# Attention followed by a mixture of experts: routing's GpSimd operations spread over the steps, and two VectorE operations fewer per routing

## The chip, the cores and the metric

The kernel runs on one core of a Trainium2 chip (trn2). The core has TensorE (PE in the profile; its weight loads are shown apart as PEld), VectorE (DVE), ScalarE (ACT), GpSimd (POOL) and SyncE (SP), which issues most of the DMAs. GpSimd issues the DMAs whose rows are addressed by an index (indirect DMAs). The metric is the device time of one execution in microseconds, lower is better.

## The reference

Four batches of 12288 queries attend to a pooled key/value image; every result row (49152 rows of 128) then goes through a gated choice of one of eight experts.

```python
kv_pool = kv.reshape(B, H // r, r, W // r, r, C).mean(axis=(2, 4))
k = v = kv_pool.reshape(B, -1, C) @ w_sr            # 768 keys per batch
a = softmax(scale * q @ k.T);  x = a @ v
do_compute = x @ w_skip > 0
logits = x[do_compute] @ w_gate                     # 8 experts
e_idx = argmax(logits);  gate_w = softmax(logits)[e_idx]
for e in range(E):                                  # rows of expert e
    y[mask] = gate_w[mask, None] * (relu(x[mask] @ w1[e]) @ w2[e])
out = x;  out[do_compute] += y
```

## The kernel before

**Steps.** The attention is one unrolled loop of 384 steps (96 per batch), one tile of 128 queries each. A step on TensorE is six score matmuls (L588 to L590, into one of two `s_ps` buffers), eighteen matmuls that apply the probabilities of the tile six steps back (`attend`, L653) and two transposes (L628). VectorE takes the row maximum of the scores (`row_max`, L596, out tile `nm`), then ScalarE the exponential (L602), then VectorE the low half of the probabilities (`p_lo`, L610, which reads two SBUF tensors); in odd steps VectorE also has L636, L661 and L663, and in every fourth step the low half of the queries (L575, two SBUF tensors). SyncE transposes the probabilities by DMA.

**Routing.** `route` is a generator for twelve tiles at a time (one `r`). A `yield 0` or `yield 3` parks it until the step number has that remainder mod 4, a bare `yield` until the next step. With `slots` (all but the last few) its parts fall into steps whose remainder mod 12 is, by r's own clock: 8 (VectorE: logits times the columns' scales, L703, and their maximum, L705; GpSimd: L707 to L723, six operations that give `d`, `ev`, `act`, `na`), 0 (VectorE L733 and L735, GpSimd the one-hot `oh_all`, L736), 3 (two matmuls that count rows, L768 and L769), 4 (VectorE L745, L774, L777, GpSimd L778 to L782, four operations) and 8 again (VectorE L784, L791, L793: the row addresses `di`; GpSimd L794 and L795). From there GpSimd issues one scatter a step for twelve steps (L184 into `scr`): each waits for that step's `row_max`. Routings overlap, so from step 32 on there is a scatter in nearly every step.

**Pooling of the next batch.** In three of four batches GpSimd also sums the key/value image of the next batch (`pool_kv`, L436 and L439), one operation a step in eight steps of twelve. Each is made to wait for the last VectorE instruction noted in `paced["both"]`, one that reads two SBUF tensors (`behind`). `KV_T` says in which step each quarter of a key/value tile is loaded.

**Order.** Each engine runs its instructions in the order in which this code emits them; nothing reorders. At step 84 of a batch the next batch's keys are made on TensorE (`prep_kv`). After the attention come the experts (from about 1080 us).

Of the kernel before, what the change touches and what calls it, by code (L numbers as in the profile page):

```python
# [9 lines left out]
F32 = mybir.dt.float32  # L10
# [14 lines left out]
def kernel(  # L25
# [343 lines left out]
    with ExitStack() as p1:  # L369
# [13 lines left out]
        def acc_ps():  # L383
            return ps_a.tile([P, 512], F32, name="acc_ps")
# [120 lines left out]
        def prep_gate():  # L505
            n = XW - C
            ps = acc_ps()
            pa = kprep.tile([P, n], F32, name="pa")
            nc.vector.scalar_tensor_tensor(out=pa, in0=proj, scalar=-1.0, in1=proj, op0=ALU.mult, op1=ALU.max)
            nc.tensor.matmul(ps[:, :n], ones_f, pa, start=True, stop=True)  # L510
            yield
            l1 = kprep.tile([P, n], F32, name="l1")
            nc.vector.tensor_copy(l1, ps[:, :n])
            inv = pow2_inverse(l1, n, gate_ds)
            nc.vector.scalar_tensor_tensor(out=pa, in0=proj, scalar=0.25, in1=inv, op0=ALU.mult, op1=ALU.mult)
            ps = acc_ps()
# [34 lines left out]
        q_sb, qT, PT, AVT, ROWS, P_SB, S_PS, P16, PTP, PTQ = ({} for _ in range(10))  # L551
        accs, scales, snaps = {}, [], []
        split_a, split_v, next_a, next_v, next_l = [], [], [], [], []
# [127 lines left out]
        def route(r, a, b, last, eng):  # L681
            n = b - a
            rows = ROWS[r][:, a:b, :]
            L = rt.tile([P, RT, E], F32, name="lg")[:, 0:n, :]
            S3 = [P, n, E]
            x_sc = KV[r * RT // TPB][5]

            def small_t(name, dt=F32):
                return rt.tile([P, RT], dt, name=name)[:, 0:n]

            def big_t(name, dt=F32):
                return rt.tile([P, RT, E], dt, name=name)[:, 0:n, :]

# [5 lines left out]

            slots = r < LASTR - 3  # L700
# [9 lines left out]
            na = small_t("na")  # L710
            few = eng is nc.vector
            if few:
                eng.scalar_tensor_tensor(out=ev, in0=d, scalar=0.0, in1=em(em8), op0=ALU.is_equal, op1=ALU.mult)
                eng.tensor_scalar(out=act, in0=rows[:, :, C], scalar1=0.0, scalar2=None, op0=ALU.is_gt)
                eng.scalar_tensor_tensor(out=na, in0=rows[:, :, C], scalar=0.0, in1=idt[:, 0:n], op0=ALU.is_le,
                                         op1=ALU.mult)
                ohb = oh_few[a // GT % 2]
            else:
                eng.tensor_scalar(out=ev, in0=d, scalar1=0.0, scalar2=None, op0=ALU.is_equal)
                eng.tensor_tensor(out=ev, in0=ev, in1=em(em8), op=ALU.mult)  # L720
                eng.tensor_scalar(out=act, in0=rows[:, :, C], scalar1=0.0, scalar2=None, op0=ALU.is_gt)
                eng.tensor_scalar(out=na, in0=act, scalar1=-1.0, scalar2=1.0, op0=ALU.mult, op1=ALU.add)
                eng.tensor_tensor(out=na, in0=na, in1=idt[:, 0:n], op=ALU.mult)  # L723
                oha = oh_all[r % 3]
                ohb = oha.rearrange("p e t -> p t e")[:, 1:RTP, :]
            yield (0 if slots else None)
            if not few and not slots:
                for _ in range(3 if r < LASTR - 1 else K1):
# [21 lines left out]
            w = n * E  # L750
            acc = big_t("acc")
            nxt = ends if last else rt.tile([P, E], F32, name="nxt")
# [12 lines left out]
            else:  # L765
# [11 lines left out]
                nc.vector.tensor_tensor(out=acc, in0=inner, in1=pre.rearrange("p e t -> p t e")[:, 0:RT, :], op=ALU.add)  # L777
                eng.tensor_tensor(out=nxt, in0=run, in1=pre[:, :, RT], op=ALU.add)  # L778
                eng.tensor_scalar(out=gs, in0=gs, scalar1=1e-9, scalar2=x_sc, op0=ALU.add, op1=ALU.mult)
                eng.tensor_tensor(out=acc, in0=acc, in1=em(run), op=ALU.add)  # L780
            accs["done"] = r * RT + b
            eng.tensor_tensor(out=acc, in0=acc, in1=ohb[:, 0:n, :], op=ALU.mult)  # L782
# [4 lines left out]
            if r == SNAPR:  # L787
                snapshot(accs["run"])
# [3 lines left out]
            di = small_t("di", I32)  # L792
            nc.vector.tensor_tensor(out=di, in0=dest, in1=na, op=ALU.add)  # L793
            nc.gpsimd.tensor_copy(rows[:, :, C + 2], x_sc.broadcast_to([P, n]))  # L794
            nc.gpsimd.iota(rows.bitcast(I32)[:, :, C + 1], pattern=[[1, n]], base=r * RT * P + a, channel_multiplier=RT)  # L795
            for j in range(n):
                if j > 0 and r < LASTR - 1:
# [135 lines left out]
        while t < NTILE + LAG - 1 or jobs:  # L933
# [44 lines left out]
            if ph == 1 and t // GT + 2 < NGRP:  # L978
                q_split(t // GT + 2)
            ranked = run_jobs(ph)  # L980
            if preps and not ranked and (ph != 0 or tb < LAG):
                if next(preps[0], "end") == "end":
                    preps.pop(0)
            if live and b + 1 < B:
                for k, r in KV_T.get(tb - 4, ()):
                    if r == R - 1:
                        pools.append(pool_kv(b + 1, k))
                if pools and next(pools[0], "end") == "end":
                    pools.pop(0)
            for _ in range(2 * (t >= NTILE)):  # L990
                next(first)
# [77 lines left out]
```

## Time and profile before

| | |
|---|---|
| median of 3 runs | 1887.3 us (1886.7 to 1890.96) |
| the profiled execution, its own time | 1881.36 us |
| its span, first to last instruction | 1878.9 us |
| PE busy | 1758.9 us, 94% |
| DVE busy | 1570.0 us, 84% |
| POOL busy | 1009.5 us, 54% |

The shares are means over the attention (to about 1030 us), a passage of some 50 us, and the experts. A stretch is read best by its own rows.

### The profile page before, as it was taken

What the parts mean: (1) busy time and instruction counts of PE and PEld (TensorE: products, weight loads), DVE (VectorE), ACT (ScalarE), POOL (GpSimd) and SP (SyncE); (2) the same over time, 40 slices, a digit from 0 to 9 for tenths busy, and PEclk for the clock granted to TensorE, in tenths of its full rate; (3) what the DMA queues carried; (4) which work ended last, traced back from release to release, by engine and by line L of the source; (5) the groups of instructions that cost most, each with busy time, mean ns of one, the idle gap of its engine ahead of it and who ended that gap; (6) DMA issues with size and microseconds to landing.
All of it is one profiled execution on the core that took longest, in us unless ns stands there. A gap on an engine that the chain in (4) does not pass through costs nothing. (4 is left out here: it accounts for less than half of the span.)

```text
span 1878.9 us, 42842 instructions
## 1 busy us (share of the span) xinstructions
PE 1758.9 (94%) x13955; PEld 1259.9 (67%) x13955; DVE 1570.0 (84%) x3322; ACT 1312.4 (70%) x2484; POOL 1009.5 (54%) x1276
## 2 busy tenths in 40 slices
PE   4999999999999999999999669999999999999997
PEld 3988889888888888899988324444444444444443
DVE  7998989998899898999997458878878877877885
ACT  3888878887878787888877236566666666666654
POOL 2168857887757888565566623433333433343343
PEclk9999999999999999999999879999999999999998
DMA  6999999999899999999998333433333333333333
GB/s 180 206 205 211 206 188 224 205 187 185 159 183 184 210 206 197 186 229 221 220 205 175 80 84 80 107 101 101 93 94 101 93 93 101 91 93 97 96 106 79
DMA packets 621972, 284.88 MB, mean 152 GB/s; under 512 B 503168, under 2 KB 571904, under 8 KB 621824
## 3 DMA queue, kind: packets, MB, share of 16 engines
q1 hardware_dynamic: 600320, 244.56, 64.6%
q0 software_dynamic: 21504, 38.43, 7.0%
q8 instruction: 82, 1.34, 0.3%
q14 instruction: 66, 0.54, 0.1%
HBM read 90.60 MB, written 78.64 MB: 90 GB/s over the span
## 5 line engine op out<-in xcount | busy, mean ns | idle before, releaser
L184 POOL DMA_INDIRECT out_dram<-o,xin x288 | 292.8, 1017 | 505.0 <-DVE o L293 438.9
L184 POOL DMA_INDIRECT scr<-rows,di x384 | 422.8, 1101 | 229.6 <-DVE nm L596 125.7
L270 DVE SCALAR_TENSOR_TENSOR h_lo<-h_ps,h_hi 128x512 f16<-128x512 f32 x544 | 341.0, 683 | 148.6 <-ACT h_hi L269 113.5
L602 ACT ACTIVATE p_sb<-s_ps,nm 128x768 f32<-128x768 f32 x384 | 346.3, 902 | 155.1 <-DVE nm L596 137.9
L596 DVE TENSOR_REDUCE nm<-s_ps 128x1 f32<-128x768 f32 x384 | 364.9, 950 | 65.4 <-PE s_ps L590 36.1
L269 ACT ACTIVATE h_hi<-h_ps 128x512 f16<-128x512 f32 x544 | 310.3, 597 | 50.5 <-PE h_ps L268 31.1
L653 PE MATMUL acc_ps<-v_hi,pt 128*128 128x138 f16 x3072 | 324.1, 225 | 18.5 <-issue 7.3
L653 PEld LDWEIGHTS <-pt 128*128 128x128 f16 x4608 | 277.6, 98 | 88.2 <-issue 82.9
L653 PE MATMUL acc_ps<-v_lo,pt 128*128 128x138 f16 x1536 | 295.3, 224 | 2.5 <-issue 2.4
L588 PE MATMUL s_ps<-k_hi,q_hi 128*128 128x384 f32 x768 | 295.4, 385 | 2.1 <-issue 2.1
L610 DVE SCALAR_TENSOR_TENSOR p<-p_sb,p 128x512 f16<-128x512 f32 x384 | 275.8, 718 | 2.6 <-DMA pt<-p 1.3
L589 PE MATMUL s_ps<-k_lo,q_hi 128*128 128x384 f32 x768 | 260.9, 340 | 0.7 <-issue 0.7
L590 PE MATMUL s_ps<-k_hi,q_lo 128*128 128x384 f32 x768 | 260.1, 339 | 1.2 <-issue 1.2
L606 ACT ACTIVATE p<-p_sb 128x512 f16<-128x512 f32 x384 | 242.4, 631 | 9.1 <-DMA pt<-p 6.2
L266 PE MATMUL h_ps<-xT,w_hi 128*128 128x512 f16 x544 | 206.8, 380 | 7.4 <-issue 7.4
L285 ACT ACTIVATE yT<-y_ps,y_sc 128x512 f32<-128x512 f32 x68 | 46.7, 687 | 230.4 <-PE y_ps L282 220.2
L267 PE MATMUL h_ps<-xT,w_hi 128*128 128x512 f16 x544 | 206.7, 380 | 0.0
L268 PE MATMUL h_ps<-xT,w_lo 128*128 128x512 f16 x544 | 206.7, 380 | 0.0
L282 PE MATMUL y_ps<-h_hi,w_hi 128*128 128x512 f16 x544 | 206.2, 379 | 0.0
L282 PE MATMUL y_ps<-h_hi,w_lo 128*128 128x512 f16 x544 | 206.2, 379 | 0.0
L282 PEld LDWEIGHTS <-w_hi 128*128 128x128 f16 x1152 | 112.8, 98 | 132.6 <-issue 0.8
L282 PE MATMUL y_ps<-h_lo,w_hi 128*128 128x512 f16 x544 | 195.1, 379 | 0.0
(208 smaller groups left out, 3128.5 us busy)
## 6 DMA issues: line engine op xcount, KB each, us to landing
kvt<-in_kv_dram SPq DMA_DIRECT2D x96, 256.0 KB
q_sb<-in_q_dram SPq DMA_DIRECT2D x96, 256.0 KB
out_dram<-rows SPq DMA_DIRECT2D x96, 256.0 KB
xin<-scr SPq DMA_DIRECT2D x75, 264.0 KB, 2.9
w_raw<-in_moe_w_dram SPq DMA_DIRECT2D x38, 512.0 KB
scr<-pad SPq DMA_DIRECT2D x32, 264.0 KB
pt<-p SPq DMA_TRANSPOSE x384
scr<-rows,di POOLq DMA_INDIRECT x384
```

Source lines behind the costliest of these rows:

```text
L184: ins = nc.gpsimd.indirect_dma_start(out=dst, out_offset=bass.IndirectOffsetOnAxis(ap=ids, axis=0), in_=src, in_offset=None, bounds_check= ...
L269: nc.scalar.activation(out=h["hi"][:, c, :], in_=ps, func=AF.Relu)
L270: nc.vector.scalar_tensor_tensor(out=h["lo"][:, c, :], in0=ps, scalar=0.0, in1=h["hi"][:, c, :], op0=ALU.max, op1=ALU.subtract)
L282: nc.tensor.matmul(ps, w[:, c, :], h[x][:, c, :], start=(i == 0), stop=(i == len(terms) - 1))
L588: nc.tensor.matmul(s[:, h, :HK], q_hi, k_hi[:, sl], start=True, stop=False)
L589: nc.tensor.matmul(s[:, h, :HK], q_hi, k_lo[:, sl], start=False, stop=False)
L590: nc.tensor.matmul(s[:, h, :HK], q_lo, k_hi[:, sl], start=False, stop=True)
L596: paced["by"] = nc.vector.tensor_reduce(out=NM[t], in_=S_PS[t][:, :, :HK], axis=AX.XY, op=ALU.max, negate=True).ins
L602: nc.scalar.activation(out=P_SB[t], in_=S_PS.pop(t)[:, :, :HK], func=AF.Exp, bias=NM.pop(t))
L606: nc.scalar.activation(out=P16[t][:, 0, :], in_=p_flat(t)[:, 0:KD * P], func=AF.Copy, scale=2.0 ** PEXP)
L610: paced["both"] = nc.vector.scalar_tensor_tensor(out=p16[:, 1, :], in0=p_flat(t)[:, 0:KD * P], scalar=2.0 ** PEXP, in1=p16[:, 0, :], op0=A ...
L653: nc.tensor.matmul(ps[:, j % 2, :], w, v[a][:, k, :], start=(i == 0), stop=(i == len(AVL) - 1))
```

## The change

Five edits. (1) The eight columns of the gate share one power of two as scale (`prep_gate`), so the logits are read straight from `rows`, the exponential takes the scale, and VectorE's L703 goes. (2) The term `na` that sends inactive rows out of bounds becomes a ninth column of `acc`, written by one GpSimd operation in place of two; VectorE takes the row address as the maximum of nine columns, straight into the integer tile `di`, in place of a sum and an addition. (3) In routings with `slots`, GpSimd's operations go through `pool`, which makes each wait for `paced["both"]` and notes it in `taken`; extra yields put at most two into a step, a step or more later than before. The scatters begin one step later (remainder 9). (4) `pool_kv` skips a step in which two were taken (until step 70 of a batch). (5) The key/value quarters are loaded every 2.5 steps in place of 3.

```diff
@@ prep_gate
             nc.vector.tensor_copy(l1, ps[:, :n])
+            nc.vector.tensor_reduce(out=l1[:, 1:2], in_=ps[:, 1:1 + E], axis=AX.X, op=ALU.max)
             inv = pow2_inverse(l1, n, gate_ds)
             nc.vector.scalar_tensor_tensor(out=pa, in0=proj, scalar=0.25, in1=inv, op0=ALU.mult, op1=ALU.mult)
+            nc.vector.tensor_scalar(out=pa[:, 1:1 + E], in0=proj[:, 1:1 + E], scalar1=inv[:, 1:2], scalar2=0.25,
+                                    op0=ALU.mult, op1=ALU.mult)
@@ route
-            L = rt.tile([P, RT, E], F32, name="lg")[:, 0:n, :]
+            def pool(name, **args):
+                op = getattr(eng, name)(**args)
+                if slots:
+                    behind(op)
+                    taken.append(name)
...
-            nc.vector.tensor_tensor(out=L, in0=rows[:, :, C + 1:C + 1 + E], in1=em(gate_ds[:, 1:1 + E]), op=ALU.mult)
+            L = rows[:, :, C + 1:C + 1 + E]
...
-            eng.tensor_tensor(out=d, in0=L, in1=bc(mx), op=ALU.subtract)
+            acc_n = big_t("acc", w=E + 1)
+            acc, na = acc_n[:, :, 0:E], acc_n[:, :, E]
+            if slots:
+                yield
+            pool("tensor_tensor", out=d, in0=L, in1=bc(mx), op=ALU.subtract)
...
+                pool("tensor_scalar", out=ev, in0=d, scalar1=0.0, scalar2=None, op0=ALU.is_equal)
+                if slots:
+                    yield
+                pool("tensor_tensor", out=ev, in0=ev, in1=em(em8), op=ALU.mult)
+                pool("tensor_scalar", out=act, in0=rows[:, :, C], scalar1=0.0, scalar2=None, op0=ALU.is_gt)
+                if slots:
+                    yield
+                pool("tensor_scalar", out=na, in0=act, scalar1=-float(BIG), scalar2=float(BIG), op0=ALU.mult,
+                     op1=ALU.add)
...
-            nc.scalar.activation(out=ex, in_=d, func=AF.Exp)
+            nc.scalar.activation(out=ex, in_=d, func=AF.Exp, scale=gate_ds[:, 1:2])
+            if slots:
+                yield 0
...
-            eng.tensor_tensor(out=ohb[:, 0:n, :], in0=oh, in1=bc(act), op=ALU.mult)
+            if slots:
+                yield
+            pool("tensor_tensor", out=ohb[:, 0:n, :], in0=oh, in1=bc(act), op=ALU.mult)
...
-            dest = small_t("dest")
-            nc.vector.tensor_reduce(out=dest, in_=acc, axis=AX.X, op=ALU.add)
             di = small_t("di", I32)
-            nc.vector.tensor_tensor(out=di, in0=dest, in1=na, op=ALU.add)
+            nc.vector.tensor_reduce(out=di, in_=acc_n, axis=AX.X, op=ALU.max)
+            if slots:
+                yield
@@ main loop
-            KV_T.setdefault(i * 3, []).append(divmod(i, R))
+            KV_T.setdefault(i * 5 // 2, []).append(divmod(i, R))
...
+            taken.clear()
...
-                if pools and next(pools[0], "end") == "end":
+                if pools and (len(taken) < 2 or tb >= 70) and next(pools[0], "end") == "end":
```

The first place where instructions move is GpSimd's queue around the start of a routing (`d` to `oh_all`; `scr` is the scatters' target, `kvt` the pooling). Before:

```order
L794 COPY rows<-x_sc 128x12
L795 IOTA rows 128x12
L184 DMA scr<-rows,di 409600x132
L707 TENSOR_TENSOR d<-lg,mx 128x96
L719 TENSOR_SCALAR ev<-d 128x96
L720 TENSOR_TENSOR ev<-ev,em_80 128x96
L721 TENSOR_SCALAR act<-rows 128x12
L722 TENSOR_SCALAR na<-act 128x12
L723 TENSOR_TENSOR na<-na,idt 128x12
L439 TENSOR_TENSOR pooled<-kvt 128x128
L184 DMA scr<-rows,di 409600x132 x4
L736 TENSOR_TENSOR oh_all_94<-oh,act 128x12x8
```

The same place on GpSimd in the changed kernel (L705 is the helper `pool`):

```order
L812 COPY rows<-x_sc 128x12
L813 IOTA rows 128x12
L184 DMA scr<-rows,di 409600x132
L705 TENSOR_TENSOR d<-rows,mx 128x96
L705 TENSOR_SCALAR ev<-d 128x96
L184 DMA scr<-rows,di 409600x132
L705 TENSOR_TENSOR ev<-ev,em_80 128x96
L705 TENSOR_SCALAR act<-rows 128x12
L184 DMA scr<-rows,di 409600x132
L705 TENSOR_SCALAR acc<-act 128x12
L436 TENSOR_TENSOR kvt<-kvt 128x256
L184 DMA scr<-rows,di 409600x132
```

Six operations and a pooling stood together ahead of four scatters in a row; now a scatter stands between every two operations, and no two scatters follow each other here.

The second place is VectorE's queue in the step with remainder 8 (`p` is `p_lo`). Before:

```order
L784 RECIPROCAL rows<-gs 128x12
L791 TENSOR_REDUCE dest<-acc 128x12
L793 TENSOR_TENSOR di<-dest,na 128x12
L703 TENSOR_TENSOR lg<-rows,gate_ds 128x96
L705 TENSOR_REDUCE mx<-lg 128x12
```

The same place on VectorE in the changed kernel:

```order
L805 RECIPROCAL rows<-gs 128x12
L809 TENSOR_REDUCE di<-acc 128x12
L714 TENSOR_REDUCE mx<-rows 128x12
L599 TENSOR_REDUCE nm<-s_ps 128x1
L639 SCALAR_TENSOR_TENSOR ptq<-acc_ps,ptq 128x512
```

Two of five routing instructions are gone there. TensorE's instructions and their order are the same in both kernels.

## Rows read from the trace of the kernel before

**Rows 1.** The page's head: span, busy time, share of the span and instructions of each engine.

```profile
span 1878.9 us, 42842 instructions
...
PE 1758.9 (94%) x13955; PEld 1259.9 (67%) x13955; DVE 1570.0 (84%) x3322; ACT 1312.4 (70%) x2484; POOL 1009.5 (54%) x1276
```

**Rows 2.** Windows of twelve steps each, cut at TensorE's first score matmul, in which TensorE waits for nothing: from:to and length in us, then busy us and instructions of PE, PEld, DVE, ACT and POOL, granted clock, the DMA engines' busy share and what they moved in GB/s. The first lies before any routing, the others hold one.

```profile
60.55:88.95 28.40, 28.40 (x314) 26.47 (x313) 25.75 (x48) 24.81 (x46) 7.81 (x14) 1.00 1.06 211
...
529.45:558.05 28.60, 28.60 (x317) 26.66 (x315) 27.52 (x57) 25.15 (x48) 16.91 (x24) 1.00 1.02 190
782.23:810.85 28.62, 28.62 (x316) 26.71 (x315) 27.73 (x57) 25.04 (x48) 17.04 (x24) 1.00 1.06 210
```

**Rows 3.** Stretches of 48, 72, 72 and 48 steps, the line of a step's first and fourth score matmuls alone (two a step): from:to, length, busy us and instructions of PE and PEld, clock, DMA.

```profile
117.53:240.85 123.32, 36.55 (x96) 18.13 (x96) 1.00 1.06 209
306.07:491.52 185.45, 54.80 (x144) 27.19 (x145) 1.00 1.02 192
558.05:744.17 186.12, 54.70 (x144) 27.19 (x144) 1.00 1.04 201
810.85:928.53 117.68, 36.53 (x96) 18.13 (x97) 1.00 1.11 222
```

**Rows 4.** Three more windows of twelve steps, columns as in the windows above: one with pooling, one without that holds the snapshot (a handful of VectorE operations more), and the one with most DMA traffic.

```profile
428.85:460.09 31.24, 29.51 (x316) 26.86 (x315) 28.19 (x56) 25.06 (x47) 25.34 (x35) 1.00 1.03 186
...
898.31:928.53 30.22, 29.10 (x317) 26.77 (x316) 27.44 (x64) 24.33 (x45) 16.75 (x25) 1.00 1.10 218
928.53:957.13 28.60, 28.60 (x315) 26.67 (x315) 28.13 (x59) 25.80 (x49) 18.30 (x26) 1.00 1.11 233
```

**Rows 5.** VectorE in order of time: start, duration, line, operation, tiles, and in brackets the idle time before and what ended it.

```profile
432.97 0.26 DVE L735 TENSOR_TENSOR oh<-em,mn 128x96 f32<-128x96 f32 x1
435.93 0.96 DVE L596 TENSOR_REDUCE nm<-s_ps 128x1 f32<-128x768 f32 x1 [2.70 <-PE s_ps L590]
...
437.73 0.69 DVE L610 SCALAR_TENSOR_TENSOR p<-p_sb,p 128x512 f16<-128x512 f32 x1
```

**Rows 6.** GpSimd in order of time over the same steps.

```profile
424.71 1.02 POOL L184 DMA_INDIRECT scr<-rows,di  x1 [0.56 <-POOL rows L795]
...
429.22 0.47 POOL L439 TENSOR_TENSOR pooled<-kvt 128x128 f32<-128x128 f32 x1
429.84 1.08 POOL L184 DMA_INDIRECT scr<-rows,di  x1 [0.16 <-DVE nm L596]
431.23 0.97 POOL L184 DMA_INDIRECT scr<-rows,di  x1 [0.30 <-issue]
432.50 1.12 POOL L184 DMA_INDIRECT scr<-rows,di  x1 [0.30 <-DVE nm L596]
433.93 0.97 POOL L184 DMA_INDIRECT scr<-rows,di  x1 [0.30 <-issue]
434.90 0.63 POOL L736 TENSOR_TENSOR oh_all<-oh,act 128x96 bf16<-128x96 f32 x1
```

**Rows 7.** GpSimd in order of time some steps earlier, between two routings' parts.

```profile
378.01 0.99 POOL L184 DMA_INDIRECT scr<-rows,di  x1 [0.17 <-issue]
...
380.34 1.19 POOL L184 DMA_INDIRECT scr<-rows,di  x1 [0.33 <-DVE nm L596]
```

**Rows 8.** TensorE in order of time (the ends of matmuls are modelled).

```profile
434.58 0.34 PE L590 MATMUL s_ps<-k_hi,q_lo 128*128 128x384 f32 x1
435.13 0.22 PE L653 MATMUL acc_ps<-v_hi,pt 128*128 128x138 f16 x1 [0.21 <-issue]
435.88 0.22 PE L653 MATMUL acc_ps<-v_hi,pt 128*128 128x138 f16 x1 [0.53 <-issue]
...
440.55 0.21 PE L768 MATMUL acc_ps<-oh_all,ones_bf 128*128 128x104 bf16 x1
```

**Rows 9.** VectorE and GpSimd together in order of time, where a pooling and a VectorE operation on two SBUF tensors meet.

```profile
353.03 0.74 POOL L436 TENSOR_TENSOR kvt<-kvt 128x256 f32<-128x256 f32 x1
...
353.11 1.20 DVE L610 SCALAR_TENSOR_TENSOR p<-p_sb,p 128x512 f16<-128x512 f32 x1
...
355.28 1.13 POOL L436 TENSOR_TENSOR kvt<-kvt 128x256 f32<-128x256 f32 x1
...
355.75 1.21 DVE L575 TENSOR_TENSOR q_lo<-q_sb,q_hi 128x512 fp32r<-128x512 f32 x1
```

**Rows 10.** The same VectorE operation where GpSimd is between scatters, in order of time.

```profile
855.85 0.69 DVE L610 SCALAR_TENSOR_TENSOR p<-p_sb,p 128x512 f16<-128x512 f32 x1
```

**Rows 11.** `row_max` in the first nine us of each of the three stretches in which the next batch's keys are made (240.85:250, 491.52:500.5 and 744.17:753): count, busy us, mean ns, and VectorE's idle us before it.

```profile
L596 DVE TENSOR_REDUCE nm<-s_ps 128x1 f32<-128x768 f32 x3 | 2.9, 951 | 3.0 <-remote 3.0
...
L596 DVE TENSOR_REDUCE nm<-s_ps 128x1 f32<-128x768 f32 x3 | 2.9, 951 | 2.7 <-remote 2.7
...
L596 DVE TENSOR_REDUCE nm<-s_ps 128x1 f32<-128x768 f32 x3 | 2.9, 951 | 2.9 <-remote 2.9
```

**Rows 12.** Groups of instructions: line, engine, operation, tiles, shapes, count, busy us, mean ns, idle us before.

```profile
L184 POOL DMA_INDIRECT scr<-rows,di x384 | 422.8, 1101 | 229.6 <-DVE nm L596 125.7 <-issue 67.5 <-DVE rs L663 8.6
...
L610 DVE SCALAR_TENSOR_TENSOR p<-p_sb,p 128x512 f16<-128x512 f32 x384 | 275.8, 718 | 2.6 <-DMA pt<-p 1.3 <-ACT p L606 1.1
...
L793 DVE TENSOR_TENSOR di<-dest,na 128x12 int32<-128x12 f32 x31 | 8.2, 265 | 1.1
...
L703 DVE TENSOR_TENSOR lg<-rows,gate_ds 128x96 f32<-128x96 f32 x31 | 7.7, 250 | 0.0
```

More of the change, by code (lines that the diff above doesn't have):

```diff
@@ L551 @@
         q_sb, qT, PT, AVT, ROWS, P_SB, S_PS, P16, PTP, PTQ = ({} for _ in range(10))
-        accs, scales, snaps = {}, [], []
+        accs, scales, snaps, taken = {}, [], [], []
         split_a, split_v, next_a, next_v, next_l = [], [], [], [], []
@@ L683, in route, with big_t @@
             rows = ROWS[r][:, a:b, :]
-            L = rt.tile([P, RT, E], F32, name="lg")[:, 0:n, :]
             S3 = [P, n, E]
             x_sc = KV[r * RT // TPB][5]
+            few = eng is nc.vector
+            slots = r < LASTR - 3
             def small_t(name, dt=F32):
                 return rt.tile([P, RT], dt, name=name)[:, 0:n]
-            def big_t(name, dt=F32):
-                return rt.tile([P, RT, E], dt, name=name)[:, 0:n, :]
+            def big_t(name, dt=F32, w=E):
+                return rt.tile([P, RT, w], dt, name=name)[:, 0:n, :]
             def bc(x):
@@ L698, in em @@
                 return x.unsqueeze(1).broadcast_to(S3)
-            slots = r < LASTR - 3
+            def pool(name, **args):
[3 more added lines that the diff above has]
+                    taken.append(name)
             if slots:
                 yield 0
-            nc.vector.tensor_tensor(out=L, in0=rows[:, :, C + 1:C + 1 + E], in1=em(gate_ds[:, 1:1 + E]), op=ALU.mult)
+            L = rows[:, :, C + 1:C + 1 + E]
             mx = small_t("mx")
@@ L706, in route @@
             d = big_t("d")
-            eng.tensor_tensor(out=d, in0=L, in1=bc(mx), op=ALU.subtract)
             ev = big_t("ev")
             act = small_t("act")
-            na = small_t("na")
-            few = eng is nc.vector
+            acc_n = big_t("acc", w=E + 1)
+            acc, na = acc_n[:, :, 0:E], acc_n[:, :, E]
+            ohb = oh_few[a // GT % 2]
+            if slots:
+                yield
+            pool("tensor_tensor", out=d, in0=L, in1=bc(mx), op=ALU.subtract)
             if few:
@@ L716, in route @@
                                          op1=ALU.mult)
-                ohb = oh_few[a // GT % 2]
             else:
[L719 to L723, printed above, removed]
+                pool("tensor_scalar", out=ev, in0=d, scalar1=0.0, scalar2=None, op0=ALU.is_equal)
[7 more added lines that the diff above has]
+                     op1=ALU.add)
                 oha = oh_all[r % 3]
                 ohb = oha.rearrange("p e t -> p t e")[:, 1:RTP, :]
-            yield (0 if slots else None)
-            if not few and not slots:
-                for _ in range(3 if r < LASTR - 1 else K1):
+            if not slots:
+                for _ in range(1 if few else 4 if r < LASTR - 1 else 1 + K1):
                     yield
             ex = big_t("ex")
-            nc.scalar.activation(out=ex, in_=d, func=AF.Exp)
+            nc.scalar.activation(out=ex, in_=d, func=AF.Exp, scale=gate_ds[:, 1:2])
+            if slots:
+                yield 0
             mn = small_t("mn")
@@ L750, in route @@
             w = n * E
-            acc = big_t("acc")
             nxt = ends if last else rt.tile([P, E], F32, name="nxt")
@@ L777, in route @@
                 nc.vector.tensor_tensor(out=acc, in0=inner, in1=pre.rearrange("p e t -> p t e")[:, 0:RT, :], op=ALU.add)
-                eng.tensor_tensor(out=nxt, in0=run, in1=pre[:, :, RT], op=ALU.add)
-                eng.tensor_scalar(out=gs, in0=gs, scalar1=1e-9, scalar2=x_sc, op0=ALU.add, op1=ALU.mult)
-                eng.tensor_tensor(out=acc, in0=acc, in1=em(run), op=ALU.add)
+                if slots:
+                    yield
+                pool("tensor_tensor", out=nxt, in0=run, in1=pre[:, :, RT], op=ALU.add)
+                pool("tensor_scalar", out=gs, in0=gs, scalar1=1e-9, scalar2=x_sc, op0=ALU.add, op1=ALU.mult)
+                if slots:
+                    yield
+                pool("tensor_tensor", out=acc, in0=acc, in1=em(run), op=ALU.add)
             accs["done"] = r * RT + b
-            eng.tensor_tensor(out=acc, in0=acc, in1=ohb[:, 0:n, :], op=ALU.mult)
+            pool("tensor_tensor", out=acc, in0=acc, in1=ohb[:, 0:n, :], op=ALU.mult)
             yield (0 if slots else None)
@@ L786, in route @@
                 yield
-            if r == SNAPR:
-                snapshot(accs["run"])
+            di = small_t("di", I32)
+            nc.vector.tensor_reduce(out=di, in_=acc_n, axis=AX.X, op=ALU.max)
+            if slots:
                 yield
-            dest = small_t("dest")
-            nc.vector.tensor_reduce(out=dest, in_=acc, axis=AX.X, op=ALU.add)
-            di = small_t("di", I32)
-            nc.vector.tensor_tensor(out=di, in0=dest, in1=na, op=ALU.add)
             nc.gpsimd.tensor_copy(rows[:, :, C + 2], x_sc.broadcast_to([P, n]))
             nc.gpsimd.iota(rows.bitcast(I32)[:, :, C + 1], pattern=[[1, n]], base=r * RT * P + a, channel_multiplier=RT)
+            if r == SNAPR:
+                yield
+                snapshot(accs["run"])
             for j in range(n):
@@ L987 @@
                         pools.append(pool_kv(b + 1, k))
-                if pools and next(pools[0], "end") == "end":
+                if pools and (len(taken) < 2 or tb >= 70) and next(pools[0], "end") == "end":
                     pools.pop(0)
+                assert not pools or tb < PREP_T
             for _ in range(2 * (t >= NTILE)):
```

## The prediction

> **What bounds the kernel now.** I read the page's head first: PE is busy for 94% of the span, DVE for 84%, POOL for 54% [rows 1]. By shares TensorE sets the time, and work that leaves VectorE or GpSimd buys nothing. But a share is a mean, so I next cut the attention into windows of twelve steps, one routing each, at TensorE's first score matmul. The quiet ones last 28.40 us before any routing and 28.60 and 28.62 with one, and in each PE is busy from end to end [rows 2]. That is TensorE's floor, 28.6 / 12 = 2.38 us a step; DVE stands close under it with 27.5 to 27.7.
>
> The other windows are longer. Four stretches of 48, 72, 72 and 48 steps take 123.32 + 185.45 + 186.12 + 117.68 = 612.57 us [rows 3]; twenty windows at the floor would be 572.0. So 40.6 us are lost there, about 2.0 a window. One window of 31.24 us has PE busy for 29.51 only [rows 4]; inside it I went to the order of time on VectorE. It ends the one-hot `oh` at 433.23 and begins the next `row_max` at 435.93, idle for 2.70 us for TensorE's scores [rows 5]. TensorE itself waits little for anything the profile names: its score matmuls and the `attend` matmuls behind them are only spaced out, with idles of 0.21 and 0.53 put down to issue [rows 8]. What is peculiar to these few us is GpSimd's queue: a pooling, then four scatters back to back, at 429.84, 431.23, 432.50 and 433.93, 1.27 to 1.43 us apart [rows 6], where normally they start 2.33 us apart [rows 7]. The reader is to see that it is catching up: the routing's six operations held the scatters behind them. I find this pairing of burst and stall in nearly every window from step 32 on; the trace shows no semaphore from a scatter to a matmul, so that the one causes the other is inferred from their coming together.
>
> Two more losses. In the three passages that make the next batch's keys, VectorE idles for 3.0, 2.7 and 2.9 us ahead of `row_max` at the same place [rows 11]. And where a pooling meets a VectorE operation on two SBUF tensors, that one takes 1.20 or 1.21 us [rows 9], against 0.69 alone [rows 10]: 0.5 us each, two a window with pooling.
>
> **The change, part by part.** *Edits 3 and 4, the spread.* No two scatters stand together any more at the place of the burst, and no more than two operations stand ahead of one. If the burst is the cause, the stall goes. Worth: the 40.6 us above; in the passages of the keys 3.0 + 2.7 + 2.9 less about 0.45 each of ordinary wait (an estimate from the shorter idles in the quiet windows) = 7.2; one more such stall at the end of the attention, taken at 1.8, a little under the 2.0 of the rest. Together 49.6. What is left of it: poolings that still meet VectorE (they did already wait behind the low halves, and two a window met it anyway); I leave 0.3 us for each of the 16 windows with pooling, 4.8. The snapshot's handful of operations, whose window lasts 30.22 [rows 4], stays at about 1.0 and something unforeseen at 0.4. Removed then: 49.6 - 6.2 = 43.4 us. The bounds: nothing (the burst is only a companion), and all 49.6.
>
> *Edits 1 and 2, two VectorE operations fewer.* L703 is 250 ns, L793 is 265 ns [rows 12]; the reduction over nine columns in place of eight, written as integers, I take at 50 ns more (96 elements a row cost L703 250 ns, so twelve more cost 31 at most; the same again for the integers makes 62, the lower bound is nothing). So 0.25 + 0.265 - 0.05 = 0.47 us a routing, 14.4 over 31. They lie beside TensorE's work, which lasts 28.6 where VectorE needs 27.7 [rows 2]: worth nothing by itself, and at most 14 us if VectorE were the bound, which only windows with collisions come near to (28.19 busy [rows 4]). I take 0 on the path, and up to 6 for the low end of the range, a bit under half, for the places where VectorE is late. The additions in `prep_gate` are two operations at the start, while loads are under way: 0. On GpSimd one operation of a routing goes, some 0.4 us of 25.34 [rows 4].
>
> *The new waits.* Every GpSimd operation of a routing now waits for VectorE's last operation on two SBUF tensors. Behind it on GpSimd's queue stand the scatters and the poolings; nobody waits for a scatter until the experts, but TensorE waits for `oh_all`. In the old window `oh_all` ends at 434.90 + 0.63 = 435.53 [rows 6] and the count that reads it begins at 440.55 [rows 8]: 5.0 us of slack. Now it goes one step later, behind the low half that ends at 437.73 + 0.69 = 438.42 [rows 5], so at about 439.1: 1.45 us are left. I take 0, with the bound in the rivals.
>
> *Edit 5, earlier loads.* Four loads in ten steps are 4.8 in twelve. The stretch with pooling moves 209 GB/s x 123.32 / 4 = 6.44 MB a window [rows 3]; a quarter is 128 keys x 4 pixels x 128 channels x 4 bytes = 0.26 MB, so 6.65 MB, and over 28.6 us 233 GB/s. One window already moved 233 with PE busy from end to end [rows 4]. So 0.
>
> *The sum.* The profiled execution took 1881.36 us. Less 43.4 it is 1838.0. It was 0.3% under the median of 1887.3; on that footing 1838.0 x 1887.3 / 1881.36 = 1843.8, say 1844 us.
>
> **The rivals.** *C: GpSimd becomes full in the windows with pooling.* Its 25.34 us of work less 0.4, and 0.16 to 0.30 ahead of each of twelve scatters [rows 4, 6], make 26.9 to 28.5 of the 28.6 that TensorE leaves. With waits for VectorE on top it may fall behind and catch up in bursts again, as before. For: the margin is thin. Against: a late GpSimd finds what it waits for done, and a scatter alone is followed by at least one operation. With the idle 31.24 - 25.34 = 5.9 us of before kept in full, nothing is gained in 16 windows; with half the stalls left the time is 1838 + 22 = 1860 and on the median's footing 1866, from 1857 to 1877.
>
> *B: the burst is not the cause.* Then the stalls move or stay, and the change is worth between nothing and the VectorE time of the windows with pooling, 0.47 x 16 = 8 us: 1873 to 1881, on the median's footing 1879 to 1887. For: bursts and stalls are tied by time alone. Against: it falls in just the steps of the burst in nearly all windows. The Trainium skill ("SBUF — State Buffer", section "SBUF: two separate sides") states that engine ports and DMA ports can't contend and that TensorE never waits on another engine at the SBUF, and by that rule spacing the scatters frees no matmul and the time would be some 1883. The trace agrees with what it says of the pair that VectorE and GpSimd share [rows 9]; on TensorE beside scatters no run here decides yet.
>
> *D: slower, TensorE waits for `oh_all`.* The slack is 1.45 us by the rows above. If GpSimd lags by more at that point, TensorE waits for the rest in each of 31 routings. It outweighs the gain from (43.4 + 3.8) / 31 = 1.5 us of wait, a lag of 3.0; at a lag of 3.5 the time is 1838 + 31 x 2.05 = 1902, or 1908. For: three steps ahead of it hold two operations and a scatter each. Against: a step's share of GpSimd's work is some 2.3 us of 2.38, so a lag of 3 must gather over many steps.
>
> *E: no effect.* The spread frees TensorE, but VectorE with its waits is late next (28.19 + 1 us of collisions that only shift), and the time stays within 0.2%.
>
> **How the numbers follow.** My chances: the forecast (A) 0.66, C 0.17, B 0.08, D 0.05, E 0.04. A by itself reaches from 1832 (49.6 and 6 us less: 1825.8 x 1.003) to 1857, where C begins. A change of 0.2%, 3.8 us, is about what a measurement of this kernel can tell from none, so B counts half as faster and half as the same: faster 0.66 + 0.17 + 0.04 = 0.87, the same 0.04 + 0.04 = 0.08, slower 0.05. The range takes in A and C and leaves B, D and E out, 0.17, and a little below: 1832 to 1878.
>
> **What would show it.** In the changed trace: every window of twelve steps near 28.6 us, those with pooling too; no two scatters of one routing closer than about 1.8 us; `row_max` waiting for scores for no more than 0.5 us at once; the low halves of the queries and of the probabilities near 0.69; the experts beginning some 44 us sooner and lasting as long as before. It is wrong if scatters are spaced and `row_max` still waits for 2 to 3 us (B), if scatters still bunch or GpSimd has no idle time in windows with pooling (C), or if TensorE's count waits for `oh_all` (D).

## The result and the profile after

The changed kernel takes 1832.78 us in the median of 4 runs (1831.83 to 1834.97), the kernel before on the same chip 1887.07: a ratio of 0.9709, interval 0.9693 to 0.9726, 54.3 us faster. The forecast was 1844, so the sign and the main loss were right and the gain came out larger by 11 us. The page's head of the changed kernel:

```profile
span 1830.0 us, 42819 instructions
...
PE 1743.1 (95%) x13955; PEld 1252.2 (68%) x13955; DVE 1561.2 (85%) x3256; ACT 1314.8 (72%) x2484; POOL 982.0 (54%) x1245
```

The profiled execution took 1831.83 us against 1881.36 before, 49.5 us less, and the span is 48.9 shorter. The same four stretches as in [rows 3], cut at the same steps (the line of the score matmuls is now L591):

```profile
116.22:232.13 115.91, 36.42 (x97) 18.13 (x97) 1.00 1.10 216
293.98:468.23 174.25, 54.81 (x144) 27.19 (x145) 1.00 1.09 206
530.16:702.17 172.01, 54.62 (x145) 27.20 (x145) 1.00 1.11 216
763.94:878.42 114.48, 36.54 (x97) 18.13 (x97) 1.00 1.14 228
```

They add up to 576.65 us, 4.65 over twenty windows at the floor of 28.6; before it was 40.6 over. That is 35.9 us of the gain. The three passages that make the next keys went from 36.57 + 37.93 + 38.06 to 33.23 + 33.35 + 33.14: 12.8 us. The last of them, before and after:

```profile
744.17:782.23 38.06, 34.72 (x341) 31.33 (x340) 32.59 (x70) 28.45 (x54) 20.80 (x32) 0.96 0.88 177
...
702.17:735.31 33.14, 32.44 (x341) 29.71 (x340) 31.45 (x67) 27.50 (x52) 19.08 (x29) 1.00 1.02 203
```

The rest of the span's 48.9 is small: 1.3 at the start, 0.8 at the end of the attention, and 2.0 lost behind it.

Three windows of twelve steps: one with pooling, to set beside the 31.24 of [rows 4], and the last two of the attention that were cut so:

```profile
587.32:615.91 28.59, 28.59 (x318) 26.66 (x316) 27.65 (x54) 24.98 (x47) 22.91 (x33) 1.00 1.13 231
...
878.42:909.11 30.69, 29.41 (x317) 26.78 (x316) 27.36 (x59) 24.41 (x46) 17.09 (x25) 1.00 1.09 219
909.11:941.95 32.84, 31.06 (x318) 28.50 (x318) 30.60 (x61) 25.60 (x48) 22.17 (x29) 0.95 1.05 217
```

In the first TensorE (28.59, the second figure) is busy from end to end with pooling and routing beside it. The other two are not: in them three and more scatters still stand together (below). The window of 30.69 answers to the one of 28.60 that stands last in [rows 4]; it became 2.1 longer, and only the one after it gained.

GpSimd in order of time at the start of a routing, to set beside [rows 6]:

```profile
318.56 1.02 POOL L184 DMA_INDIRECT scr<-rows,di  x1 [0.91 <-POOL rows L813]
319.60 0.37 POOL L705 TENSOR_TENSOR d<-rows,mx 128x96 f32<-128x96 f32 x1
320.06 0.47 POOL L705 TENSOR_SCALAR ev<-d 128x96 f32<-128x96 f32 x1
320.85 1.06 POOL L184 DMA_INDIRECT scr<-rows,di  x1 [0.32 <-issue]
322.33 0.38 POOL L705 TENSOR_TENSOR ev<-ev,em 128x96 f32<-128x96 f32 x1 [0.42 <-DVE q_lo L578]
...
323.32 1.06 POOL L184 DMA_INDIRECT scr<-rows,di  x1 [0.38 <-DVE nm L599]
```

The scatters start 2.29 and 2.47 us apart where they stood 1.27 to 1.43 apart. Two groups of VectorE, all of the attention: `row_max` in the kernel before and in the changed one, with the idle time before it in the last figures, and the low half of the probabilities, which had a mean of 718 ns [rows 12]:

```profile
L596 DVE TENSOR_REDUCE nm<-s_ps 128x1 f32<-128x768 f32 x384 | 364.9, 950 | 65.4 <-PE s_ps L590 36.1 <-PE acc_ps L653 13.1 <-remote 11.2
...
L599 DVE TENSOR_REDUCE nm<-s_ps 128x1 f32<-128x768 f32 x384 | 364.9, 950 | 21.2 <-PE s_ps L593 9.7 <-issue 4.9 <-PE acc_ps L656 4.3
L613 DVE SCALAR_TENSOR_TENSOR p<-p_sb,p 128x512 f16<-128x512 f32 x384 | 285.6, 744 | 8.8 <-ACT p L609 6.6 <-DMA pt<-p 0.9 <-issue 0.6
```

VectorE stands idle 44 us less before `row_max`; waits of over 1 us went from 26 to 2. The low half of the probabilities did not become shorter, as forecast, but longer (744 ns); the low half of the queries went from 773 to 720 ns, short of the forecast 690.

### The profile page after: what moved, and what is told of

Same layout as the page of the kernel before. It is cut to its first block, busy times and chain, and to the rows that moved or that the text cites. A ratio compares the mean times of both kernels' runs of the same rounds, so it can differ in the third digit from the quotient of the medians.

```text
span 1830.0 us, 42819 instructions
## 1 busy us (share of the span) xinstructions
PE 1743.1 (95%) x13955; PEld 1252.2 (68%) x13955; DVE 1561.2 (85%) x3256; ACT 1314.8 (72%) x2484; POOL 982.0 (54%) x1245
## 5 line engine op out<-in xcount | busy, mean ns | idle before, releaser
L184 POOL DMA_INDIRECT scr<-rows,di x384 | 417.3, 1087 | 203.5 <-DVE nm L599 129.1
L591 PE MATMUL s_ps<-k_hi,q_hi 128*128 128x384 f32 x768 | 294.0, 383 | 0.0
L613 DVE SCALAR_TENSOR_TENSOR p<-p_sb,p 128x512 f16<-128x512 f32 x384 | 285.6, 744 | 8.8 <-ACT p L609 6.6
L285 ACT ACTIVATE yT<-y_ps,y_sc 128x512 f32<-128x512 f32 x68 | 46.7, 687 | 227.4 <-PE y_ps L282 227.4
```

The lines of the kernel that those rows point to most:

```text
L184: ins = nc.gpsimd.indirect_dma_start(out=dst, out_offset=bass.IndirectOffsetOnAxis(ap=ids, axis=0), in_=src, in_offset=None, bounds_check= ...
L591: nc.tensor.matmul(s[:, h, :HK], q_hi, k_hi[:, sl], start=True, stop=False)
L613: paced["both"] = nc.vector.scalar_tensor_tensor(out=p16[:, 1, :], in0=p_flat(t)[:, 0:KD * P], scalar=2.0 ** PEXP, in1=p16[:, 0, :], op0=A ...
```

## Experiments

The kernels below ran on three chips, and on each the kernel before ran beside them, so only ratios to it are compared across chips. It took 1880.08 us on the chip of the first four kernels, 1884.93 on that of the next four and 1822.01 on that of the last four; the last chip turned out to matter, and is dealt with at the end of this section.

**A burst put back.** Everything spread, but four of the twelve scatters in one step:

```diff
+            STEPS = (0, 1, 2, 3, 4, 5, 5, 5, 5, 9, 10, 11)
...
-                if j > 0 and r < LASTR - 1:
+                if slots:
+                    for _ in range(STEPS[j] - STEPS[max(j - 1, 0)]):
+                        yield
+                elif j > 0 and r < LASTR - 1:
                     yield
```

> The changed kernel with four of a routing's twelve scatters issued in one step (remainder 2, after the one-hot), everything else spread as it is. If scatters back to back stall TensorE (the theory), row_max waits some 2 to 2.5 us for scores once per routing, at remainder 2 to 3 and no longer at 11 or 0: 31 x 2.0 to 2.4 = 62 to 75 us more than the changed kernel, 1895 to 1908. If the burst was only a companion of the late routing operations or of VectorE's collisions (the rival), nothing but the poolings behind it moves: 1830 to 1840.

Measured: 1853.79 us, ratio 0.9862 (0.9834 to 0.9890), so 1.5% or 29 us more than the changed kernel's 0.9709. GpSimd around one burst of this kernel, then the last score matmul on TensorE and the `row_max` that reads it:

```profile
668.48 1.01 POOL L184 DMA_INDIRECT scr<-rows,di  x1 [0.16 <-DVE nm L599]
669.80 0.97 POOL L184 DMA_INDIRECT scr<-rows,di  x1 [0.30 <-issue]
671.07 1.08 POOL L184 DMA_INDIRECT scr<-rows,di  x1 [0.30 <-DVE nm L599]
672.45 0.97 POOL L184 DMA_INDIRECT scr<-rows,di  x1 [0.31 <-issue]
```

```profile
671.36 0.34 PE L593 MATMUL s_ps<-k_hi,q_lo 128*128 128x384 f32 x1
...
674.52 0.96 DVE L599 TENSOR_REDUCE nm<-s_ps 128x1 f32<-128x768 f32 x1 [2.44 <-remote]
```

The trace names no releaser for this wait (`remote`), but `row_max` reads only the scores. By the trace, which models the ends of matmuls, these were done at 671.36 + 0.34 = 671.70, 2.8 us before `row_max` could start; an ordinary wait for scores ends 0.04 us behind their last matmul. In the kernel before this delay was 1.5 to 3.7 us at the stalls. The stall is back, and it has moved with the burst, four steps later in the twelve: 33 of the 34 runs of three or more close scatters in this kernel's attention are followed by a step of `row_max` over 3 us (25 of 27 in the kernel before). So bursts cause it on these chips. But the price was half of what the theory gave: its windows with pooling lasted 29.1 to 30.4 us, 0.5 to 1.8 over the floor and not 2.0 to 2.4. The wait of 2.44 us is one of the two longest; after most bursts `row_max` waited only 0.8 to 1.2 us and came 3.1 to 3.6 us after the one before it (2.4 is normal), where the kernel before mostly had waits of 2.6 to 3.1 and steps of 4.6 to 5.1. The same burst costs less here, and no run shows why.

**Two pairs in place of four.** `STEPS = (0, 1, 2, 3, 4, 5, 5, 7, 7, 9, 10, 11)`.

> The changed kernel with two pairs of scatters per routing (remainders 2 and 4), nothing else changed. If every scatter that follows another at once costs the same (a burst of four holds three such, so 2.3 / 3 = 0.75 us each), two pairs cost 1.5 a routing: +46, 1879. If a stall needs a longer burst, as the pairs in the changed kernel's trace suggest (a step of 3.0 to 3.4 at most), 0 to 20 us: 1833 to 1853.

Measured: 1831.61 us, ratio 0.9743 (0.9724 to 0.9762), 0.3% or 6 us over the changed kernel, and the intervals touch; on this same chip it is 22 us below the kernel with the burst of four. Two in a row are nearly free; it takes more of them.

**The arithmetic alone.** The kernel before with edits 1 and 2 (two VectorE operations and one GpSimd operation fewer per routing); the added yields, waits, skips and earlier loads are left out:

```diff
-            nc.vector.tensor_tensor(out=L, in0=rows[:, :, C + 1:C + 1 + E], in1=em(gate_ds[:, 1:1 + E]), op=ALU.mult)
+            L = rows[:, :, C + 1:C + 1 + E]
...
-            dest = small_t("dest")
-            nc.vector.tensor_reduce(out=dest, in_=acc, axis=AX.X, op=ALU.add)
             di = small_t("di", I32)
-            nc.vector.tensor_tensor(out=di, in0=dest, in1=na, op=ALU.add)
+            nc.vector.tensor_reduce(out=di, in_=acc_n, axis=AX.X, op=ALU.max)
```

> The kernel before with edits 1 and 2 alone: two VectorE operations and one GpSimd operation fewer a routing, nothing spread, loads every three steps. Theory (TensorE's floor and the bursts set the time): the bursts stay, 0 to 8 us less, 1879 to 1887. Rival (VectorE sets it): 14 us less or more, 1873 or below.

Measured: 1861.81 us, ratio 0.9911 (0.9891 to 0.9931): 16.7 us less than before, beyond the upper end of my theory and at the rival's figure. The step "I take 0 on the path" fell. A window of the kernel before that is not among the rows above, and VectorE's only idle times over 0.1 us in it, suggest why:

```profile
588.24:619.71 31.47, 29.41 (x316) 26.89 (x316) 28.17 (x57) 25.16 (x47) 25.36 (x34) 1.00 0.96 188
```

```profile
L596 DVE TENSOR_REDUCE nm<-s_ps 128x1 f32<-128x768 f32 x13 | 12.3, 948 | 3.0 <-PE s_ps L590 3.0
L663 DVE RECIPROCAL rs<-rs 128x2 f32<-128x2 f32 x6 | 1.0, 166 | 0.2
```

VectorE is busy for 28.17 us and stands still for 3.2, most of it in the one stall: 31.4 of 31.47. Outside the stall it hardly waits. So it was VectorE that set this window's length: TensorE's late scores held it for 3 us, then TensorE delivered and VectorE worked off what had piled up at its own pace until the next burst. In such a window work taken from VectorE shortens the window, and a stall adds to it. A window of the kernel with the arithmetic alone agrees, with 0.39 us less of VectorE's work, a stall 0.2 shorter and 0.65 less in all:

```profile
608.27:639.09 30.82, 29.28 (x318) 26.73 (x316) 27.78 (x54) 25.28 (x47) 25.14 (x33) 1.00 1.17 209
```

This is not the whole of the 16.7 us: `row_max` also waited over 1 us only 18 times in place of 26, 42.4 us in place of 56.9. Edit 2 takes an operation from GpSimd too, and this run does not separate the two. Nor does time to spare on VectorE explain the cheaper bursts of the first experiment: a window of that kernel without pooling, with VectorE busy for 26.63 us only, is still 1.0 us over the floor:

```profile
781.99:811.61 29.62, 28.82 (x317) 26.70 (x315) 26.63 (x53) 25.00 (x46) 16.95 (x24) 1.00 1.12 215
```

**The spread alone.** The kernel before with seven more yields, in routings with `slots`, and nothing else:

```diff
+            if slots:
+                yield
             eng.tensor_tensor(out=d, in0=L, in1=bc(mx), op=ALU.subtract)
```

> The kernel before with the extra yields alone: routing's GpSimd operations at most two a step, without the waits for VectorE, without the skipped poolings, VectorE's operations and the loads as before. Theory: the bursts go and with them most of the loss; collisions of GpSimd with VectorE's two-SBUF operations stay and grow: 30 to 46 us less than before, 1841 to 1857. Rival (the waits or the two VectorE operations carry the gain): less than 20 us, 1867 or more.

Measured: 1841.51 us, ratio 0.9802 (0.9783 to 0.9821), 37 us (1.98%) of the 54. Together with the arithmetic's 0.89% that is 2.87%, against the whole change's 2.91%. `row_max` waits over 1 us only twice in this kernel, as in the changed one. Its four stretches, of the same steps as in [rows 3]:

```profile
116.88:232.85 115.97, 36.43 (x96) 18.12 (x97) 1.00 1.10 222
295.36:471.29 175.93, 54.81 (x145) 27.20 (x145) 1.00 1.07 203
533.81:709.80 175.99, 54.65 (x144) 27.19 (x145) 1.00 1.10 212
772.32:887.23 114.91, 36.55 (x97) 18.12 (x97) 1.00 1.15 228
```

They are 10.8 us over the floor, 29.8 less than before, and the passages of the keys last 33.9 each, 10.9 less together. The arithmetic alone left the same stretches 25.3 over, 15.3 less.

**All but the arithmetic.** The changed kernel with edits 1 and 2 undone, so L703, the sum and the addition are back, and GpSimd's second operation for `na`:

> The changed kernel with edits 1 and 2 undone: L703 and L793 back on VectorE, one more operation on GpSimd, all else as changed. Edits 1 and 2 alone were worth 0.9% of the kernel before. Theory: they were worth that because VectorE ran late behind the bursts and could not catch up; with the bursts gone TensorE is at its floor and VectorE has 28.6 - 28.2 to spare, so undoing them costs 0 to 8 us over the changed kernel: ratio to the kernel before 0.971 to 0.976. Rival: VectorE's operations count in full everywhere, 14 to 17 us: 0.979 or more.

Measured: 1853.18 us, ratio 0.9826 (0.9812 to 0.9839). The two operations are worth 1.2% with the bursts gone too (against the changed kernel's 0.9709; 1.05% against the 0.9721 of the next kernel, which ran on this same chip), about 20 us, more than the 16 to 17 of their old durations. A window with pooling and one of the last batch, which pools nothing:

```profile
627.72:657.75 30.03, 28.97 (x316) 26.81 (x316) 29.69 (x56) 24.94 (x47) 24.04 (x34) 1.00 1.12 237
...
782.25:810.87 28.62, 28.62 (x318) 26.69 (x316) 27.43 (x56) 24.99 (x47) 17.48 (x26) 1.00 1.19 223
```

With pooling VectorE is busy for 29.69 of 30.03 us and sets the time without any burst; without pooling TensorE does, at its floor. The two operations themselves got longer:

```profile
L811 DVE TENSOR_TENSOR di<-dest,na 128x12 int32<-128x12 f32 x31 | 11.0, 356 | 1.1
L709 DVE TENSOR_TENSOR lg<-rows,gate_ds 128x96 f32<-128x96 f32 x31 | 10.1, 327 | 0.0
```

These are 356 and 327 ns against 265 and 250 in [rows 12]. Most of them last as before; four of `lg` take about 850 ns and eight of `di` 628 to 705, so single meetings with GpSimd's work are the likely reason.

**Without the new waits.** `behind(op)` left out of `pool`.

> The changed kernel without the new waits: a routing's GpSimd operations don't wait for VectorE's last operation on two SBUF operands. Theory: more collisions of about 0.5 us on VectorE, which has little to spare in windows with pooling: 3 to 12 us over the changed kernel, ratio to the kernel before 0.972 to 0.977, and the low halves' means above 0.744 and 0.72 us. Rival: the waits only cost GpSimd time: as fast as the changed kernel or up to 4 us faster, 0.969 to 0.971.

Measured: 1833.90 us, ratio 0.9721 (0.9708 to 0.9734): not to be told from the changed kernel, nor were the low halves longer (741 and 725 ns against 744 and 720). The waits do nothing that can be measured.

**Loads every three steps.** `KV_T.setdefault(i * 3, ...)`.

> The changed kernel with the key/value quarters loaded every 3 steps, as before. Theory (no engine waits for these loads): within 4 us of the changed kernel, 0.969 to 0.973. Rivals: the denser loads delay the transposes of the probabilities, which ScalarE waits for in the second batch's windows of 29.2 us (then 2 to 4 us faster, 0.967 to 0.969), or poolings come too late for the next batch's keys (then slower by 5 us or more).

Measured: 1834.24 us, ratio 0.9725 (0.9712 to 0.9738): no difference that can be told.

**No skipped poolings.** The condition on `taken` left out.

> The changed kernel in which a pooling is also issued in steps that already took two routing operations. Theory: three operations in a step make GpSimd late by under a scatter, so that some scatters follow at 1.4 us and collisions grow: 2 to 10 us over the changed kernel, 0.972 to 0.976. Rival: GpSimd has room and the skip is worth nothing, 0.970 to 0.972.

Measured: 1836.81 us, ratio 0.9737 (0.9724 to 0.9750). At most 5 us of the gain are the skip's, and the intervals touch.

**The last four kernels ran on a chip that behaves differently.** On it the kernel before takes 1822.01 us. First, the burst in the kernel without the arithmetic (the STEPS of the first experiment in the fifth kernel):

> The burst of four at remainder 2 put into the kernel without edits 1 and 2. Theory (a window with pooling lasts what VectorE is busy plus what it stood still for TensorE's late scores, so a stall counts in full where VectorE has nothing to spare): the burst costs 2.0 us in each of 16 windows with pooling, 2.5 in three prep passages and 4 elsewhere, 43 us over the kernel without the edits: ratio to the kernel before 1.003 or more. Rival (a burst costs the same whatever VectorE has to do): 29 us, as on the changed kernel: 0.998 or less.

Measured: 1829.35 us, ratio 1.0049 (1.0035 to 1.0064). By the number the theory would be borne out, but the trace forbids that reading. GpSimd and VectorE of this kernel:

```profile
456.09 1.01 POOL L184 DMA_INDIRECT scr<-rows,di  x1 [0.16 <-DVE nm L596]
457.40 0.97 POOL L184 DMA_INDIRECT scr<-rows,di  x1 [0.30 <-issue]
458.67 1.06 POOL L184 DMA_INDIRECT scr<-rows,di  x1 [0.30 <-issue]
460.04 0.97 POOL L184 DMA_INDIRECT scr<-rows,di  x1 [0.30 <-issue]
```

```profile
459.37 0.32 DVE L792 TENSOR_TENSOR acc<-acc_ps,pre 128x96 f32<-128x96 f32 x1
459.60 0.96 DVE L596 TENSOR_REDUCE nm<-s_ps 128x1 f32<-128x768 f32 x1
460.47 0.69 DVE L636 SCALAR_TENSOR_TENSOR ptq<-acc_ps,ptq 128x512 f16<-128x512 f32 x1
```

The same four scatters at the same spacing of 1.27 to 1.37 us, and `row_max` follows the operation before it at once. It is so throughout: only 4 of the 33 runs of three or more scatters are followed by a long step, and `row_max` stands idle for 11.3 us in the whole attention, never for 1 us at once, against 65.4 in the kernel before on its chip. On this chip a burst doesn't hold TensorE up. The ratio is over 1, then, probably because the kernel before has little to lose there; no trace of that kernel on this chip was kept. Whether a burst costs more where VectorE is fuller was not told apart by this run.

The chips differ in another place too. From the last `row_max` to the first matmul of the experts' main loop, the kernels on the other chips take 93 to 96 us and the four here 79 to 81; ScalarE waits there once for 18 to 20 us (L285) on the others, and here for 6.2 at most. So some 15 of the 60 us by which the kernel before is faster here are probably not in the steps of the attention. No run shows the cause.

Second, two VectorE operations per routing whose results nobody reads, of one SBUF operand each, added to the changed kernel:

```diff
+            if slots:
+                nc.vector.tensor_scalar(out=big_t("lg"), in0=L, scalar1=0.5, scalar2=None, op0=ALU.mult)
...
+            if slots:
+                nc.vector.tensor_scalar(out=small_t("dest"), in0=acc_n[:, :, E], scalar1=0.5, scalar2=None, op0=ALU.mult)
```

> The changed kernel with two idle VectorE operations per routing where L703 and the sum stood, of one SBUF operand each, so that they take VectorE's time (about 0.4 us together) and can't meet GpSimd's. Theory (the two removed operations were worth their time on VectorE): 10 to 20 us over the changed kernel, ratio to the kernel before 0.976 to 0.982. Rival (they were worth their collisions with GpSimd, being operations on two SBUF operands): 0 to 6 us, 0.970 to 0.974.

Measured: 1818.47 us, ratio 0.9986 (0.9975 to 0.9998). The changed kernel itself had no run on this chip; the first of the two kernels below, which differs from it in one late routing, took 1811.38, so the two operations cost about 7 us. They took 378 and 188 ns in the mean, 0.566 x 28 = 15.8 us of VectorE's time, and about half of it counted, between the two theories. But this run does not tell time from collisions, because the operations met GpSimd's work after all. The durations (least, median, longest) of the two show it, and so does the second beside a pooling, where it takes 0.55 us in place of 0.11:

```profile
L714 DVE TENSOR_SCALAR lg<-rows x28: 193/314/658, 82.2 to 876.8; 128x96 f32<-128x96 f32 x28
L812 DVE TENSOR_SCALAR dest<-acc x28: 102/109/558, 110.9 to 905.9; 128x12 f32<-128x12 f32 x28
```

```profile
139.98 1.18 POOL L436 TENSOR_TENSOR kvt<-kvt 128x256 f32<-128x256 f32 x1
...
140.63 0.55 DVE L812 TENSOR_SCALAR dest<-acc 128x12 f32<-128x12 f32 x1
```

The five longest of the second, 0.55 to 0.56 us, all lie beside a pooling like this one; the 22 that lie beside a scatter took 0.10 to 0.11.

Third and fourth, `slots` for one and for two routings more (`r < LASTR - 2`, `r < LASTR - 1`). They were made for these rows of the changed kernel, three scatters behind five operations in a row and the wait that follows, in the window of 30.69 us shown above:

```profile
900.97 1.08 POOL L184 DMA_INDIRECT scr<-rows,di  x1 [0.58 <-DVE nm L599]
902.35 0.98 POOL L184 DMA_INDIRECT scr<-rows,di  x1 [0.30 <-issue]
903.63 0.97 POOL L184 DMA_INDIRECT scr<-rows,di  x1 [0.30 <-issue]
```

```profile
905.46 0.22 DVE L664 TENSOR_SCALAR rs<-acc_ps,v_sc 128x2 f32<-128x2 f32 x1 [2.22 <-PE acc_ps L631]
```

> The changed kernel with the spread also for the fourth-last routing (slots one routing longer). In the changed trace that routing still does five operations in a row ahead of three scatters, and a step of 5.29 us follows. Theory (the burst makes the stall): that step goes to about 2.4, 2 to 3 us faster than the changed kernel, ratio 0.969 to 0.970. Rival: the step stays long, or the later scatters move a loss to the start of the experts: 0.971 or more.

> The same for the fourth- and third-last routings. In the changed trace the third-last one is followed by steps of 4.72, 4.07 and 3.70 us around scatters 1.3 to 1.4 us apart. Theory: 4 to 7 us faster than the changed kernel, ratio 0.967 to 0.969. Rival: the last scatters end later than the attention and the experts wait for them: 0.971 or more.

Measured: 1811.38 us, ratio 0.9945 (0.9933 to 0.9958), and 1812.34 us, ratio 0.9950 (0.9937 to 0.9962). The window that answers to the one of 30.69 us lasted 29.04 and 29.05, but on a chip on which bursts don't stall TensorE this proves nothing, and neither kernel can be set beside the changed one. What they do show is what is left of the gain on this chip: 0.5 to 0.6%, some 10 us, in place of 54.

## Why the prediction was right, and where its sum was off

**Right: the bursts.** The largest loss was found by cutting the attention into windows of twelve steps and asking what stood beside each stall. A kernel with a burst put back at another place has the stall at that place, though at half the price; a kernel with the spread alone gains 37 us. The term for the four stretches said 40.6 - 6.2 = 34.4; the spread alone took 29.8 of it, and the whole change 35.9.

**Off: VectorE's two operations at 0.** With the GpSimd operation that goes with them they are worth 16.7 us alone and about 20 on top of the rest. The step that failed reads "They lie beside TensorE's work, which lasts 28.6 where VectorE needs 27.7 [rows 2]: worth nothing by itself". That compared quiet windows without pooling. Of the windows with pooling I had the number, VectorE busy for 28.19, and read it as only near the bound of 28.6; but that window lasted 31.24, and 28.19 + 2.70 [rows 4, 5] nearly fill it. Adding the engine's busy time and its idle time in one window would have suggested that VectorE set it. The rival B counted this time where A did not.

**Close by luck.** That my sum came within 6 us of the profiled gain (43.4 against 49.5) although it left out 17 to 20 us has a plain reason: I had credited the whole excess over the floor to the bursts, and the excess was the bursts' and VectorE's together. One error made up for the other. The spread alone leaves VectorE in charge of the windows with pooling, as this one of that kernel shows (29.41 busy of 29.75):

```profile
619.86:649.61 29.75, 29.14 (x317) 26.79 (x316) 29.41 (x56) 24.91 (x47) 26.50 (x34) 1.00 1.14 232
```

**Off: the passages of the keys.** 12.8 us in place of 7.2. I had priced them by the idle time of `row_max` alone; they got shorter by 3.3 to 4.9 each. That TensorE's clock no longer fell may account for some of it: the two that gained 4.6 and 4.9 had a granted clock of 0.96 in the kernel before, the one that gained 3.3 had 1.00, and all three have 1.00 now.

**Off: the footing.** I scaled the profiled time up by 0.3% to reach the median. The changed kernel's profiled execution is 0.95 us under its median, the one before was 5.7 under; that difference, 4.8 of the 54.3 us, lies between single executions of a kernel and says nothing of the change.

**The rivals.** C (GpSimd full) fell: it is busy for 22.91 of 28.59 us with pooling, down from 25.34, more than the one operation that went; the poolings on `kvt` took 731 ns each in the mean where they took 858, and the comparison `ev` 471 where it took 911. Over the whole attention not every operation became shorter: `oh_all` went from 629 to 679 ns. D (TensorE waits for `oh_all`) fell: it waited 0.8 us for it in the whole attention. B fell on the chips of 1880 to 1887 us: there a burst put back brought the stall back, with a wait of 2.44 us in the rows above. On the chip of 1822 us it did not. By the Trainium skill ("SBUF — State Buffer", section "SBUF: two separate sides") TensorE waits for no other engine at the SBUF. What I had drawn from this beside B, that spacing scatters frees no matmul, came out wrong on the first chips; the page speaks of the SBUF's ports, and no run shows whether TensorE was held up there. Edit 5, the waits and the skip are worth nothing to 5 us, as taken, but the low halves did not go to 0.69: the mean of the probabilities' rose from 718 to 744 ns, probably because poolings that no longer lag run beside them.

## What to carry to other kernels

For each window add an engine's busy and idle time: the engine that has no idle time but the stall sets the window, and then work taken from it can shorten it, however the average shares look. When stalls name no culprit, list what happens in the steps of the stall and nowhere else, and then move that one thing: the stall moves with the cause. Try to space one engine's transfers, and don't let them pile up behind a block of its own arithmetic.

## What the runs showed of the hardware

- Four scatters issued by GpSimd 1.27 to 1.4 us apart held back TensorE's results on the chips that run the kernel before in 1880 to 1887 us. In the kernel before VectorE mostly waited 2.6 to 3.1 us for them where pooling ran (2.70 and 2.95 above); after the bursts put back it waited 0.8 to 1.2 us in most places and 1.9 to 2.5 in some; behind three in the changed kernel it waited 2.22. Two in a row cost almost nothing. The way in which they do so stays open: no wait in the trace links them, the granted clock is 1.00 in those windows, and the score matmuls themselves are recorded as done 1.3 to 3.7 us before VectorE can read them (0.04 us at an ordinary wait).
- On the chip of the last four kernels the same burst held nothing back. The kernel before runs there in 1822 us, 3.3% faster than the 1885 on the chip of the four kernels ahead of them; some 15 us of that probably lie behind the attention. Two kernels close to the changed one gain 0.5% on it, a fifth of what the change is worth elsewhere. A gain of this kind should be measured on more than one chip.
- A VectorE operation of one SBUF operand can be lengthened by GpSimd too: `dest<-acc` took 0.55 to 0.56 us beside a pooling and 0.10 to 0.11 beside a scatter.
